# DeltaNet followed by soft MoE: products leave PSUM by ScalarE alone, masks are applied later in SBUF, both state copies run on ScalarE, and the routing exponentials are taken on transposed logits

## The chip, the cores and the metric

The kernel runs on one core of a Trainium2 chip. The metric is the device time of one execution in microseconds (us). Before the change three runs took 434.18, 437.84 and 441.81 us, so the median is 437.84.

## The reference

Two blocks stand one behind the other. The first is a DeltaNet recurrence over B = 4 batches, H = 8 heads, S = 768 steps and head size D = 48; for every batch and head it carries a 48x48 state:

```python
k_n = k / (norm(k, axis=-1) + 1e-6)
for t in range(S):
    y[t]  = q[t] @ state
    v_old = k_n[t] @ state
    state = state + beta[t] * outer(k_n[t], v[t] - v_old)
x = y as (B*S, H*D)                      # 3072 tokens x 384
```

The second is a soft mixture of experts on these 3072 tokens, with 8 experts of 4 slots each (32 slots) and a hidden size F = 1024:

```python
logits = x @ phi                                   # 3072 x 32
d = softmax over tokens of logits                  # per slot
slot_out = relu((d.T @ x)[expert e] @ w1[e]) @ w2[e]
c = softmax over slots of logits                   # per token
out = c @ slot_out                                 # 3072 x 384
```

## The kernel before

**Chunks and groups.** The recurrence is cut into 24 chunks of C = 32 steps. Within a chunk it is written as a small triangular system, so that only the state has to pass from chunk to chunk. Four chunks make a group (GC = 4, NG = 6 groups); the 128 partitions are 4 heads x 32 steps, and U = 8 pairs of a batch and a half of the heads lie side by side in the free dimension.

**What is done ahead of a chunk.** `prep(cc)` runs LEAD = 8 chunks ahead. It transposes K and Q on TensorE (L173) into PSUM, ScalarE copies them out (KQ, L176), and TensorE multiplies keys with keys and with queries (L188) into two PSUM banks. ScalarE takes the key-key half out (Lc, L194), and VectorE the query-key half, times the triangular mask `tri` (AT, L195). Once four chunks of a group are there, `invert(n)` solves their triangular systems together: VectorE transposes Lc into lb (L207), the norms follow (L221 to L229, with a square root on ScalarE), GpSimd scales lb (L230), and 31 elimination steps of two VectorE instructions each follow, a product pr (L240) and a subtraction from tt (L243). GpSimd scales tt (L247), and VectorE transposes it into TT (L253).

**A chunk itself.** TensorE multiplies the state with the keys (psR, L278), VectorE forms R = V - psR (L286), TensorE multiplies R with the inverse (psW, L297), ScalarE copies that to U (L300), TensorE adds to the state in PSUM (psS, L308), and the new state S is copied to SBUF in two halves: ScalarE takes the first (L320), VectorE the second (L318). The outputs (psY, L326) leave by ScalarE (Y, L329). GpSimd scales V two chunks ahead by the norms (L259).

**Routing.** After a group, `route` turns Y on TensorE (L350, copied by L351 to yT), forms logits (L359, copied to lT by L363), turns them to tokens (copied by VectorE to lg, L368), takes maxima and exponentials by slots and by tokens, and adds the weighted tokens to the running sum sacc (slots, L431 on TensorE and L439 on VectorE). One group's routing is spread over the four chunks of the next group.

**What sets the order.** Each engine executes its instructions in the order in which the program issues them, and between `tc.manual_schedule()` and its end that is the order of the code. A loop over x = -8 .. 23 issues, per chunk, `rest`, `scale_v`, `read`, then the pieces of `prep` and, between them, five places (PLACES = 5). Each place takes some elimination steps of the next group, as the table `share` gives them, and some steps of the routing:

```python
rest(); scale_v(x + 2); read()
x0(); place(0); solve(); x1(); place(1)
update(); outputs(); place(2); xp(); place(3); place(4)
```

**PSUM and queues.** Of the eight banks two belong to the tag pt (transposes, products, routing), one to psRW (psR and psW), one to psY and four to psS. K, Q and V are loaded over SyncE's queue, twelve chunks ahead for K and Q; Q of chunks 0 and 1 go over ScalarE's queue, beta and phi over GpSimd's.

**Behind the recurrence.** The expert weights w1 of experts 0 and 1 are loaded early. All others are issued by SyncE behind the recurrence (L152, L156), into buffers that use the recurrence's memory, so that each waits until that memory is free. First products (ph, L589) and second products (pso, L613) run over experts 0 to 3, then 4 to 7; then the output is formed and stored.

## Time and profile before

| what | value |
| --- | --- |
| median of 3 runs | 437.84 us (434.18 to 441.81) |
| the profiled execution's own time | 437.39 us |
| its span, first to last instruction | 435.7 us |
| mean granted TensorE clock | 0.855 |
| TensorE busy (matmuls / weight loads) | 299.1 / 227.6 us |
| VectorE busy | 248.9 us, 679 instructions |
| ScalarE busy | 129.1 us, 257 instructions |
| GpSimd busy | 63.5 us, 88 instructions |

The profile is that of one execution. A row of the groups view names the line of the code, the engine (PE is TensorE, PEld its weight loads, DVE VectorE, ACT ScalarE, POOL GpSimd, SP SyncE, SPq SyncE's queue of transfer issues), the operation, output and inputs with their shapes, the count, the busy time and the mean of one in ns, and the idle time ahead of them with what ended it. A waits row reads "who waited <- for whom: total us, times, longest". The span is 1.69 us shorter than the execution's own time.

### The profile page before, as it was taken

The numbers are of one execution on the slowest core, as the hardware profiler recorded it, in microseconds if no ns is written. First come the engines' busy times: TensorE is split into PE (matmuls) and PEld (weight loads), VectorE is DVE, ScalarE is ACT, GpSimd is POOL, SyncE is SP. The second block draws the span as 40 slices with busy tenths as digits, with TensorE's granted clock in tenths as the row PEclk, the third lists the DMA queues.
The fourth block names the chain that finished last, engine by engine and source line by source line (L and its number), as shares of the span: only waits on it lengthen the run. The fifth ranks groups of instructions, "written<-read, shape, count | busy, mean of one in ns | idle before, by whom it ended". The sixth has DMA issues, their size and how long they took to land. (4 is left out here: it accounts for less than half of the span.)

```text
span 435.7 us, 20600 instructions
## 1 busy us (share of the span) xinstructions
PE 299.1 (69%) x9387; PEld 227.6 (52%) x9387; DVE 248.9 (57%) x679; ACT 129.1 (30%) x257; POOL 63.5 (15%) x88
## 2 busy tenths in 40 slices
PE   3563547765686777857768767864777786887584
PEld 2452436654575656746656656654666664432142
DVE  4137978688868767586575875778752312111033
ACT  2242213233453224532154414323223221111022
POOL 8203034003300133000330013300130000000000
PEclk9999999799998697986699758867699697999695
DMA  6555955444432233223011100103100079879347
GB/s 109 98 90 88 320 83 86 76 83 81 71 54 37 43 58 59 42 43 53 4 21 24 21 10 16 22 3 105 46 5 5 3 245 428 346 294 426 148 152 283
DMA packets 84759, 45.53 MB, mean 105 GB/s; under 512 B 79392, under 2 KB 82624, under 8 KB 82624
## 3 DMA queue, kind: packets, MB, share of 16 engines
q1 hardware_dynamic: 81920, 43.67, 36.7%
q8 instruction: 74, 1.21, 1.1%
q10 hardware_dynamic: 2176, 0.39, 0.5%
q0 software_dynamic: 576, 0.15, 0.3%
q14 instruction: 13, 0.11, 0.1%
HBM read 39.47 MB, written 4.72 MB: 101 GB/s over the span
## 5 line engine op out<-in xcount | busy, mean ns | idle before, releaser
L240 DVE TENSOR_TENSOR pr<-tt,lb 128x31 f32<-128x31 f32 (+15 forms) x186 | 68.5, 368 | 9.5 <-POOL lb L230 4.7
L243 DVE TENSOR_TENSOR tt<-tt,pr 128x31 f32<-128x31 f32 (+15 forms) x186 | 68.2, 367 | 6.4
L173 PE MATMUL pt<-ident,K 128*128 128x128 f32 x96 | 34.3, 371 | 26.6 <-DVE AT L195 21.0
L176 ACT ACTIVATE KQ<-pt 128x512 f32<-128x512 f32 x48 | 28.5, 595 | 67.5 <-PE pt L173 67.5
L297 PE MATMUL psW<-R,TT 32*32 32x48 f32 x1536 | 25.8, 224 | 28.6 <-DVE R L286 28.0
L297 PEld LDWEIGHTS psW<-R,TT 32*32 32x32 f32 x1536 | 22.1, 122 | 34.4 <-DVE R L286 31.4
L318 DVE COPY S<-psS 48x768 f32<-48x768 f32 x23 | 22.1, 960 | 31.4 <-ACT S L320 31.4
L188 PE MATMUL pt<-KQ 48*32 48x64 f32 x1536 | 30.7, 263 | 11.9 <-issue 5.5
L173 PEld LDWEIGHTS pt<-ident,K 128*128 128x128 f32 x96 | 17.0, 178 | 32.7 <-DVE AT L195 23.3
L173 PE MATMUL pt<-ident,Q 128*128 128x128 f32 x96 | 32.2, 348 | 0.9 <-issue 0.9
L188 PEld LDWEIGHTS pt<-KQ 48*32 48x32 f32 x1536 | 21.9, 125 | 20.4 <-ACT KQ L176 8.7
L326 PE MATMUL psY<-U,AT 32*32 32x48 f32 x1536 | 26.4, 219 | 5.4 <-issue 5.3
L278 PE MATMUL psY<-S,KQ 128*32 128x96 f32 x768 | 28.8, 306 | 1.1 <-issue 1.1
L278 PE MATMUL psR<-S,KQ 128*32 128x96 f32 x768 | 29.4, 310 | 0.2
L431 PE MATMUL pt<-Y,dr 32*32 32x97 f32 x768 | 24.4, 278 | 6.7 <-issue 3.5
L247 POOL TENSOR_TENSOR tt<-tt,gm 128x1024 f32<-128x1024 f32 x6 | 11.5, 1912 | 103.0 <-DVE tt L243 89.9
L195 DVE TENSOR_TENSOR AT<-pt,tri 128x128 f32<-128x128 f32 x48 | 12.0, 289 | 25.0 <-ACT Lc L194 24.7
L326 PEld LDWEIGHTS psY<-U,AT 32*32 32x32 f32 x1536 | 21.8, 117 | 8.1 <-issue 6.4
L278 PEld LDWEIGHTS psY<-S,KQ 128*32 128x32 f32 x768 | 24.9, 144 | 1.5 <-issue 1.3
L278 PEld LDWEIGHTS psR<-S,KQ 128*32 128x32 f32 x768 | 23.1, 141 | 4.3 <-issue 2.6
L431 PEld LDWEIGHTS pt<-Y,dr 32*32 32x32 f32 x768 | 20.6, 123 | 9.1 <-issue 4.6
L194 ACT ACTIVATE Lc<-pt 128x128 f32<-128x128 f32 x48 | 14.6, 405 | 33.2 <-PE pt L188 33.2
(124 smaller groups left out, 440.4 us busy)
## 6 DMA issues: line engine op xcount, KB each, us to landing
w1t<-in_moe_w_dram SPq DMA_DIRECT2D x8, 1536.0 KB, 8.4
w2t<-in_moe_w_dram SPq DMA_DIRECT2D x8, 1536.0 KB, 14.1
K<-in_k_dram SPq DMA_DIRECT2D x96, 48.0 KB, 2.4
V<-in_v_dram SPq DMA_DIRECT2D x96, 48.0 KB, 2.3
out_dram<-ob SPq DMA_DIRECT2D x24, 192.0 KB, 2.3
Q<-in_q_dram SPq DMA_DIRECT2D x88, 48.0 KB, 2.7
Q<-in_q_dram ACTq DMA_DIRECT2D x8, 48.0 KB, 2.9
bb<-in_beta_dram POOLq DMA_DIRECT2D x16, 6.0 KB, 2.8
```

The costliest lines, as they stand in the source:

```text
L173: nc.tensor.transpose(tp[:, i, a, :], src[:, b * G:(b + 1) * G, :].rearrange("p g d -> p (g d)"), ident)
L176: nc.scalar.activation(KQ[cc][:, 2 * bh:2 * bh + 2], tp, ACT.Copy)
L188: nc.tensor.matmul(pg[g][rh, b], lhsT=KQ[cc][r, b, 0, rh], rhs=KQ[cc][r, b, :, rh], start=True, stop=True, skip_group_check=True)
L194: nc.scalar.activation(by[:, c, g], pg[g][:, :, 0, :], ACT.Copy)
L195: nc.vector.tensor_tensor(AT[cc][:, g], pg[g][:, :, 1, :], tri.unsqueeze(1).broadcast_to([P, B, C]), op=ALU.mult)
L240: nc.vector.tensor_tensor(prv, tt[:, j, 0:m].unsqueeze(1).broadcast_to([P, w, m]), lb[:, j, j + 1:C].unsqueeze(2).broadcast_to([P, w, m]), ...
L243: nc.vector.tensor_tensor(tt[:, j + 1:C, 0:m], tt[:, j + 1:C, 0:m], prv, op=ALU.subtract)
L278: nc.tensor.matmul(dst[hs[h], b].rearrange("p g d -> p (g d)"), lhsT=kq[:, b, a, hs[h]], rhs=old[:, h, b, :], start=(b == 0), stop=False, ...
L297: nc.tensor.matmul(pw[hs[h], u], lhsT=T[hs[h], u], rhs=st["R"][hs[h], u], start=(u == 0), stop=True, skip_group_check=True)
L318: nc.vector.tensor_copy(dst, src)
L326: nc.tensor.matmul(st["py"][hs[h], b, g], lhsT=at[hs[h], g, b], rhs=st["U"][hs[h], b * G + g], start=False, stop=True, skip_group_check=True)
L431: nc.tensor.matmul(pa[r], lhsT=st["dr"][r, c, b, :], rhs=Yn[r, c, b, 0:GD + 1], start=(b == 0), stop=(b == B - 1), skip_group_check=True)
```

## The change

- **Products and masks.** ScalarE copies both halves of the products together into a new tile GQ (128x256, two copies per chunk instead of two plus two). VectorE masks the query-key half later, in SBUF, with one instruction of 128x256 per chunk (`mask`, new L207), which is placed in the next chunk behind its first elimination steps.
- **State copies.** Both halves run on ScalarE (new L334).
- **Elimination.** The transpose to lb reads GQ with a stride and is issued at the end of the chunk before the group that it belongs to; the square root goes with it. GpSimd's scalings of lb and tt and the transpose to TT are each cut into two halves. `share` has four places per chunk, and the first chunk of a group takes 0.14 of the work (0.17 before), the next two 0.28 (0.31), the last 0.30 (0.23).
- **Routing.** Y is turned chunk by chunk (`turn`, four batches of one chunk, instead of one batch of four chunks), one chunk later. The maxima over tokens come from the transposed logits lT; the exponentials over tokens are taken on lT (dT) with the negative running maximum as bias, and those over slots straight from PSUM, with their sums by the same instruction (`accum_out`), four instructions of ScalarE. VectorE's copies and subtractions for them go. `slots` takes two chunks at a time.
- **Lead-in.** The eight steps x < 0 have a loop of their own. The order of the loads changes: Q1 moves from ScalarE's queue to SyncE's, K3 and Q3 from SyncE's to GpSimd's, and the masks are built ahead of beta and phi. A square root on a constant is put ahead of everything on ScalarE. Transposes in the lead-in use the banks psRW and psY.

```diff
+    one = cpool.tile([P, 1], F32, name="one")
+    nc.vector.memset(one, 1.0)
+    root = small.tile([P, 1], F32, name="root", tag="root", bufs=1)
+    nc.scalar.activation(root, one, ACT.Sqrt)
     load_k(0)
     load_q(0, nc.scalar)
-    load_k(1)
-    load_q(1, nc.scalar)
...
-    load_k(3)
-    load_q(3)
+    load_k(3, nc.gpsimd)
+    load_q(3, nc.gpsimd)
...
         def transposes(bh):
...
+            if cc < LEAD:
+                tag = ("psRW", "psY")[bh]
+                tp = ps.tile([P, 2, 2, P], F32, name="tp", tag=tag)
+            else:
+                tp = pt([P, 2, 2, P])
...
-            by = Lc[n].rearrange("p t (c b g) -> p c g b t", c=GC, b=B)
             for g in range(G):
-                nc.scalar.activation(by[:, c, g], pg[g][:, :, 0, :], ACT.Copy)
-                nc.vector.tensor_tensor(AT[cc][:, g], pg[g][:, :, 1, :],
-                                        tri.unsqueeze(1).broadcast_to([P, B, C]), op=ALU.mult)
+                nc.scalar.activation(GQ[n][:, c, :, g], pg[g], ACT.Copy)
+
+        def mask():
+            a = GQ[n][:, c, :, :, 1, :].rearrange("p b g t -> p (b g) t")
+            nc.vector.tensor_tensor(a, a, tri.unsqueeze(1).broadcast_to([P, U, C]), op=ALU.mult)
...
-            nc.vector.transpose(lb.rearrange("p t s -> p (t s)"),
-                                Lc.pop(n).rearrange("p t c -> p (t c)"))
+            nc.vector.transpose(
+                lb, GQ[n].rearrange("p c b g a t -> p a t (c b g)")[:, 0])
...
-            nc.gpsimd.tensor_tensor(st["lb"], st["lb"],
-                                    gm.unsqueeze(2).broadcast_to([P, C, C]), op=ALU.mult)
+            for r in (slice(0, C // 2), slice(C // 2, C)):
+                nc.gpsimd.tensor_tensor(
+                    st["lb"][:, r], st["lb"][:, r],
+                    gm[:, r].unsqueeze(2).broadcast_to([P, C // 2, C]), op=ALU.mult)
...
-                dst = new[r, :, :, g * D:(g + 1) * D]
-                src = psS[r, :, 0:B * D].rearrange("p h (b d) -> p h b d", d=D)
-                if g:
-                    nc.vector.tensor_copy(dst, src)
-                else:
-                    nc.scalar.activation(dst, src, ACT.Copy)
+                nc.scalar.activation(
+                    new[r, :, :, g * D:(g + 1) * D],
+                    psS[r, :, 0:B * D].rearrange("p h (b d) -> p h b d", d=D), ACT.Copy)
...
+        def over_slots():
...
+            nc.vector.tensor_reduce(mx, st["pq"], axis=AX.X, op=ALU.max, negate=True)
+            for b in range(B):
+                nc.scalar.activation(el[:, b], st["pq"][:, b], ACT.Exp, bias=mx[:, b:b + 1],
+                                     accum_out=sm[:, b:b + 1])
...
+        def spread_max():
...
+            dT = st["dT"] = wk.tile([P, P], F32, name="dT", tag="dT", bufs=1)
+            nc.scalar.activation(dT, st["lT"], ACT.Exp, bias=new)
...
-    PLACES = 5
+    PLACES = 4
-    share = [(0.0, 0.0, 0.05, 0.05, 0.07), (0.05, 0.06, 0.06, 0.06, 0.07),
-             (0.05, 0.06, 0.06, 0.06, 0.07), (0.08, 0.08, 0.07, 0.0, 0.0)]
+    share = [(0.0, 0.06, 0.06, 0.02), (0.10, 0.08, 0.08, 0.02),
+             (0.10, 0.08, 0.08, 0.02), (0.14, 0.10, 0.06, 0.0)]
...
         rest()
         scale_v(x + 2)
         read()
         x0()
+        if x > 0:
+            turn(i, Ys[m % 2], yT[m])
-        place(0)
+        drain(EL[c][0])
+        drain(masks)
         solve()
         x1()
+        routing[c][0][0]()
-        place(1)
+        drain(EL[c][1])
+        routing[c][0][1]()
         update()
         outputs()
-        place(2)
+        drain(EL[c][2])
         xp()
-        place(3)
-        place(4)
+        routing[c][1][0]()
+        drain(EL[c][3])
+        routing[c][1][1]()
+        masks = [mask]
+        if c == GC - 1 and n + 2 < NG:
+            spread, EL = plan(n + 2)
+            spread()
```

Three places show how the instructions move. The rows give the line, the operation, output and inputs and the shape; pr and tt are the elimination's two instructions.

**VectorE, second chunk of a group**, before: from R (in the first row) on through the state copy, the two masked products and the routing's copy lg.

```order
L286 TENSOR_TENSOR R<-V,psR 128x384
L240 TENSOR_TENSOR pr<-tt,lb 128x192
L243 TENSOR_TENSOR tt<-tt,pr 128x24x8
L240 TENSOR_TENSOR pr<-tt,lb 128x207
L243 TENSOR_TENSOR tt<-tt,pr 128x23x9
L240 TENSOR_TENSOR pr<-tt,lb 128x220
L243 TENSOR_TENSOR tt<-tt,pr 128x22x10
L318 COPY S_180<-psS 48x16x48
L240 TENSOR_TENSOR pr<-tt,lb 128x231
L243 TENSOR_TENSOR tt<-tt,pr 128x21x11
L195 TENSOR_TENSOR AT<-pt,tri 128x128 x2
```

Now, from R of the same chunk on (the mask L207, the routing's maximum over rows L409):

```order
L305 TENSOR_TENSOR R<-V,psR 128x384
L255 TENSOR_TENSOR pr<-tt,lb 128x175
L258 TENSOR_TENSOR tt<-tt,pr 128x25x7
L255 TENSOR_TENSOR pr<-tt,lb 128x192
L258 TENSOR_TENSOR tt<-tt,pr 128x24x8
L255 TENSOR_TENSOR pr<-tt,lb 128x207
L258 TENSOR_TENSOR tt<-tt,pr 128x23x9
L207 TENSOR_TENSOR GQ<-GQ,tri 128x8x32
L409 TENSOR_REDUCE mr<-pt 1x32
L255 TENSOR_TENSOR pr<-tt,lb 128x220
```

The state copy and the products out of PSUM are gone from VectorE's list; the mask, on SBUF alone, stands behind three elimination steps, ahead of a reduction that reads PSUM.

**ScalarE, the same chunk**, before (KQ and Lc of the chunk eight ahead, U, S and Y of this one, lT and yT of the routing):

```order
L176 ACTIVATE KQ<-pt 128x512
L300 ACTIVATE U<-psW 128x384
L176 ACTIVATE KQ<-pt 128x512
L351 ACTIVATE yT<-pt 96x4x4x32
L320 ACTIVATE S_180<-psS 48x16x48
L329 ACTIVATE Y_187<-psY 128x4x96
L363 ACTIVATE lT<-pt 128x128
L194 ACTIVATE Lc<-pt 128x4x32 x2
```

and now (el and sm are the exponentials over slots and their sums; ACT_TABLE_LOAD fetches another function's table):

```order
L186 ACTIVATE KQ<-pt 128x512
L361 ACTIVATE yT<-pt 96x16x32
L319 ACTIVATE U<-psW 128x384
L186 ACTIVATE KQ<-pt 128x512
L334 ACTIVATE S_184<-psS 48x16x48 x2
L345 ACTIVATE Y_192<-psY 128x4x96
L202 ACTIVATE GQ<-pt 128x4x64 x2
L393 ACT_TABLE_LOAD
L393 ACTIVATE el,sm<-pt,mx 128x32 x4
```

S has two copies in a row, GQ takes the place of Lc with twice the size, yT stands ahead of U, and four exponentials stand at the chunk's end.

**VectorE at a group's end**, before (sacc are the additions of the routing, TT the transposed inverse of the next group, R the first subtraction of that group, lb the transpose for the group after it):

```order
L240 TENSOR_TENSOR pr<-tt,lb 128x31
L243 TENSOR_TENSOR tt<-tt,pr 128x31
L439 TENSOR_TENSOR sacc<-sacc,pt 128x97
L195 TENSOR_TENSOR AT<-pt,tri 128x128 x2
L439 TENSOR_TENSOR sacc<-sacc,pt 128x97
L253 STREAM_TRANSPOSE TT<-tt 128x32x32
L439 TENSOR_TENSOR sacc<-sacc,pt 128x97
L286 TENSOR_TENSOR R<-V,psR 128x384
L207 STREAM_TRANSPOSE lb<-Lc 128x1024
L221 TENSOR_SCALAR ssq<-lb 128x32
```

and now:

```order
L255 TENSOR_TENSOR pr<-tt,lb 128x31
L258 TENSOR_TENSOR tt<-tt,pr 128x31
L272 STREAM_TRANSPOSE TT<-tt 128x16x32
L456 SCALAR_TENSOR_TENSOR sacc<-sacc,al,pt 128x97
L218 STREAM_TRANSPOSE lb<-GQ 128x1024
L229 TENSOR_SCALAR ssq<-lb 128x32
L305 TENSOR_TENSOR R<-V,psR 128x384
L236 RECIPROCAL rn<-nrm 128x32
```

Only half of TT stands behind the last elimination step (the first half is transposed a chunk earlier), and the transpose to lb with the squares ssq has moved from behind R to ahead of it.

More of the change, by code (lines that the diff above doesn't have):

```diff
@@ new lines, in shares, with over_rows @@
+        def shares():
+            sm = st["sm"]
+            nc.vector.tensor_scalar(sm, sm, 1e-9, None, op0=ALU.add)
+            nc.vector.reciprocal(sm, sm)
+            nc.gpsimd.tensor_tensor(Call[:, n], st["el"],
+                                    sm.unsqueeze(2).broadcast_to([P, B, NSL]), op=ALU.mult)
+        def over_rows():
+            pm = pt([1, B, NSL])
+            nc.tensor.transpose(pm.rearrange("p b s -> p (b s)"), st["m1"], ident)
+            mr = st["mr"] = small.tile([1, NSL], F32, name="mr", tag="mr")
+            nc.vector.tensor_reduce(mr, pm.rearrange("p b s -> p s b"), axis=AX.X, op=ALU.max)
@@ L388, in over_tokens @@
+        def spread_max():
+            pb = pt([P, 1])
+            for b in range(B):
+                nc.tensor.matmul(pb[C * b:C * b + C], lhsT=st["mr"], rhs=one[0:1],
+                                 start=True, stop=True, skip_group_check=True)
+            new, old = nrun[n % 2], nrun[1 - n % 2]
             if n == 0:
-                nc.vector.tensor_reduce(mrun, pm, axis=AX.X, op=ALU.max)
+                nc.vector.tensor_scalar(new, pb, -1.0, None, op0=ALU.mult)
             else:
-                m1 = small.tile([P, 1], F32, name="m1", tag="m1")
+                nc.vector.scalar_tensor_tensor(new, pb, -1.0, old, op0=ALU.mult, op1=ALU.min)
@@ L392, in over_tokens @@
                 al = st["al"] = small.tile([P, 1], F32, name="al", tag="al")
[L393 to L395 removed]
+                nc.vector.tensor_tensor(al, new, old, op=ALU.subtract)
                 nc.scalar.activation(al, al, ACT.Exp)
[L397 to L404 removed]
@@ L439, in slots @@
                 nc.vector.tensor_tensor(sacc, sacc, pa, op=ALU.add)
-        return ([lambda b=b: turn(b) for b in range(B)]
-                + [logits, by_tokens, maxima, over_tokens, shares, weights, repeat]
-                + [lambda c=c: slots(c) for c in range(GC)])
+        no = nothing
+        return [[(logits, no), (no, maxima)],
+                [(over_rows, no), (by_tokens, over_slots)],
+                [(no, no), (spread_max, shares)],
+                [(repeat, no), (lambda: slots((0, 1)), lambda: collect(True))],
+                [(no, no), (lambda: slots((2, 3)), lambda: collect(False))]]
+    nothing = lambda: None
     def drain(*lists):
```

268 lines of the change are left out of this document (142 added, 126 removed).

## The prediction

> **What bounds the kernel now.** I cut the span first into four stages, at VectorE's subtractions R (one per chunk of 32 steps), because every chunk of the recurrence passes through R. The rows of the windows view give, after start, end and length, the busy time and count on TensorE, its weight loads, VectorE, ScalarE and GpSimd, then the granted clock, the DMA share and GB/s.
>
> ```profile
> 0.00:64.50 64.50, 31.74 (x644) 24.48 (x644) 36.55 (x112) 17.56 (x36) 20.01 (x40) 1.00 0.64 132
> 64.50:322.30 257.80, 182.22 (x7116) 152.45 (x7116) 187.52 (x503) 87.63 (x170) 42.25 (x44) 0.82 0.24 45
> 322.30:348.80 26.50, 21.13 (x844) 17.80 (x848) 8.15 (x21) 9.30 (x18) 0.40 (x1) 0.84 0.01 4
> 348.80:435.70 86.90, 63.98 (x791) 32.88 (x783) 16.63 (x47) 14.61 (x33) 0.84 (x4) 0.85 0.74 291
> ```
>
> A, 64.5 us, is the lead-in up to the first R. B, 257.8 us, holds 20 chunks, during which the next group's elimination runs. C is three further intervals without elimination, D everything behind the last R. B decides. There VectorE is busy for 187.5 of 257.8 us and TensorE for 182.2, so neither is full, and the next question is what VectorE waits for. The waits view of stage B (total us, times, longest):
>
> ```profile
> DVE S L318 <- ACT S L320: 22.9, 19, 2.9
> DVE AT L195 <- ACT Lc L194: 12.4, 10, 2.4
> DVE R L286 <- PE psR L278: 9.8, 6, 2.2
> DVE TT L253 <- POOL tt L247: 4.0, 3, 1.7
> DVE sacc L439 <- PE pt L431: 3.6, 3, 1.4
> DVE rn L223 <- ACT nrm L222: 3.4, 5, 1.7
> DVE pr L240 <- POOL lb L230: 2.8, 4, 0.8
> PE psW L297 <- DVE R L286: 26.4, 10, 4.1
> ```
>
> VectorE's seven waits make 58.9 us; the remaining 11.4 us are the small gaps between its 503 instructions. It takes its list in order, so while it stands before the state copy S or the products AT, the elimination steps behind them stand too; so does the next R, for which TensorE in turn waits 26.4 us. That is my reading of B: VectorE's list, busy time plus waits, sets the pace. The chain that ended last reaches back only to 344.5 us and speaks for D alone.
>
> **B, part by part.** Durations come from the groups view (count | total us, mean ns | idle before):
>
> ```profile
> L318 DVE COPY S<-psS 48x768 f32<-48x768 f32 x23 | 22.1, 960 | 31.4 <-ACT S L320 31.4
> L320 ACT ACTIVATE S<-psS 48x768 f32<-48x768 f32 x23 | 18.5, 803 | 10.1 <-PE psS L308 9.7
> L195 DVE TENSOR_TENSOR AT<-pt,tri 128x128 f32<-128x128 f32 x48 | 12.0, 289 | 25.0 <-ACT Lc L194 24.7
> L240 DVE TENSOR_TENSOR pr<-tt,lb 128x256 f32<-128x256 f32 x6 | 2.5, 421 | 0.0
> L207 DVE STREAM_TRANSPOSE lb<-Lc 128x1024 f32<-128x1024 f32 x6 | 7.4, 1228 | 0.0
> L253 DVE STREAM_TRANSPOSE TT<-tt 128x1024 f32<-128x1024 f32 x6 | 11.8, 1961 | 4.0 <-POOL tt L247 4.0
> L439 DVE TENSOR_TENSOR sacc<-sacc,pt 128x97 f32<-128x97 f32 x18 | 4.5, 253 | 9.0 <-PE pt L431 8.7
> L397 DVE COPY mrun<-m 128x1 f32<-128x1 f32 x5 | 0.7, 147 | 0.1
> ```
>
> State copies: 20 x 0.960 = 19.2 us leave VectorE, and the wait of 22.9 us with them. On ScalarE both halves take 2 x 0.803 = 1.61 us, against 0.803 + 0.960 now, so the state is not later.
>
> Masks: 32 products of 0.289 us (9.2 us) go, with their wait of 12.4 us. In come 16 masks on 128x256 in SBUF, which no row shows; the elimination's 128x256 product at 0.421 is nearest, the two old products at 0.578 bound it above and one, 0.289, below. I take 0.421: 6.7 us, net -2.5 (-4.6 to 0). A mask is placed behind the next chunk's first elimination steps, when its copy is long done. ScalarE's copy doubles to 128x256, between its old 128x128 and a 128x512; it replaces two, so I add nothing.
>
> Routing: 17 groups of VectorE instructions, from L439 with the most time to L397 with the least, make 24.7 us for six groups, 4.1 each. Nine remain for each group; at a mean of 0.24 us, between 0.147 and 0.4, they make 2.2 (1.3 to 3.6). Four groups lie in B: -7.8 us (-11 to -2).
>
> The transpose to lb reads with a stride now. Contiguous it took 1.228, the transpose TT that writes with a stride 1.961; I take the slower: 4 x 1.96 - 5 x 1.23 = +1.7 us, since the one for group 1 moves into A (-1.2 to +4).
>
> Halves: GpSimd's scalings of lb and tt are cut in two so that VectorE starts after the first. Whether that gains is seen where GpSimd works beside VectorE:
>
> ```profile
> 224.37 1.62 POOL L259 TENSOR_TENSOR V<-V,nT 128x384 f32<-128x384 f32 x2
> 224.45 0.80 DVE L240 TENSOR_TENSOR pr<-tt,lb 128x31 f32<-128x31 f32 x1 [0.76 <-POOL lb L230]
> 60.19 0.19 DVE L240 TENSOR_TENSOR pr<-tt,lb 128x31 f32<-128x31 f32 x1
> ```
>
> The same product took 0.80 us beside GpSimd and 0.19 alone. A second half of about 1 us would hold VectorE up again; two such places in five groups cost 0 to 8 us, and I take 5. [...]
>
> Busy: 187.5 - 19.2 - 2.5 - 7.8 + 1.7 + 5 = 164.7 us. Gaps: about 440 instructions instead of 503, so 10. The waits for R, TT, sacc, rn and lb I keep: 23.6. That makes 198.3 us.
>
> What comes late next is R waiting for psR. How long a chunk takes without elimination is seen in C:
>
> ```profile
> 322.31 0.52 DVE L286 TENSOR_TENSOR R<-V,psR 128x384 f32<-128x384 f32 x1
> 328.37 0.56 DVE L286 TENSOR_TENSOR R<-V,psR 128x384 f32<-128x384 f32 x1 [1.27 <-PE psR L278]
> 337.83 0.56 DVE L286 TENSOR_TENSOR R<-V,psR 128x384 f32<-128x384 f32 x1
> 348.25 0.56 DVE L286 TENSOR_TENSOR R<-V,psR 128x384 f32<-128x384 f32 x1 [3.74 <-issue]
> ```
>
> So 6.1 to 10.4 us; I take 8. The list per chunk is 198.3 / 20 = 9.9 us on average and covers it, but the new shares put only 0.14 of the elimination into a group's first chunk, whose list comes to some 6.5 us: 1.5 us in five groups, 7.5 us. For the new reductions that wait for TensorE I add 2.2. **B: 208 us.** Its ends: 186, if halves cost nothing and half of the waits for TensorE go; 237, if the 35.3 us of S and AT come back before R and the halves cost 8.
>
> **A.** The queue rows carry this, with the first lb and the first elimination step:
>
> ```profile
> 0.81 7.57 SPq L80 DMA_DIRECT2D K<-in_k_dram  x12
> 8.42 1.93 SPq L80 DMA_DIRECT2D Q<-in_q_dram  x4
> 27.96 1.23 DVE L207 STREAM_TRANSPOSE lb<-Lc 128x1024 f32<-128x1024 f32 x1
> 35.28 0.80 DVE L240 TENSOR_TENSOR pr<-tt,lb 128x31 f32<-128x31 f32 x1 [1.91 <-POOL lb L230]
> ```
>
> SyncE issues twenty loads for chunks 0 to 2 instead of K0 to K3 and two Q; by these rows the last, Q2, is out at 0.81 + 7.57 + 2 x 1.93 = 12.2 us and lands, an estimate, near 15. K3 and Q3 go over GpSimd, ahead of beta, which is needed only for the norms. From 15 us I allow TensorE 10 for three chunks' transposes and products, now without the wait for the mask: lb at 25 instead of 28, and by the shorter norms (no table load, half a scaling) the first step at 30.3. From there it was 29.2 us to R; the transpose of group 1 (2.2) and the halves (1.6) come in, about 1 us of scaling goes: 32.2. **A: 62.5** (58 to 68; the upper end if GpSimd's eight issues delay what stands behind them).
>
> **C and D.** C loses turns and VectorE's copy: 24.5 (20.5 to 28.5). D is bound by weights:
>
> ```profile
> 355.14 2.13 SPq L156 DMA_DIRECT2D w2t<-in_moe_w_dram  x4
> 383.87 7.69 SPq L156 DMA_DIRECT2D w2t<-in_moe_w_dram  x4
> 391.18 17.68 DMA w2t<-in_moe_w_dram
> ```
>
> The last six loads wait for buffers that the first expert product frees, at 383, and land at 408.9, 25 us later; the loads before them are issued from 355.1, 7 us behind the last R. The routing chain after the recurrence has one turn instead of four and fewer VectorE steps, some 4 us less; but the earlier six loads need their 25 us too, from 7.5 us behind R, so the last lands no sooner than 57.5 behind it, against 60.6 now. **D: 83.8** (79 to 87).
>
> Sum: 62.5 + 208 + 24.5 + 83.8 = 378.8, and 1.7 us around the span, as now (437.39 - 435.70): **380 us**. The profiled 437.39 stands 0.45 below the median shown, 437.84, so nothing is corrected for.
>
> **Rivals.**
>
> TensorE at half clock remains the pace. For: it is busy as long as VectorE, and each long wait sends it to half clock:
>
> ```profile
> 275.37 0.88 PE L297 MATMUL psW<-R,TT 32*32 32x48 f32 x64
> 286.50 1.50 PE L297 MATMUL psW<-R,TT 32*32 32x48 f32 x64 [4.05 <-DVE R L286]
> ```
>
> The same 64 instructions took 1.50 after 4.05 us of idleness. Its work hardly shrinks: 182 us plus waits of 45 is B = 227, in all 400 us. Chance 0.18.
>
> TensorE stays at full clock. With 15 to 35 us fewer idle, chunks in the chain come nearer to 6.1 us, B falls to its lower end, 186, and the time to 358: 0.15. [...]
>
> The freed waits only change their name: R waits for psR as long as S and AT were waited for, and the masks, exponentials and ScalarE's longer queue take the rest. The work then brings nothing: 430 to 440 us, 0.04.
>
> Slower: ScalarE as the only exit from PSUM. Its exponentials stand ahead of the next chunk's KQ, yT and U, wait for a VectorE maximum, and hold the bank that TensorE's next turn needs, ahead of psW. Against: busy 87.6 + 20 x 0.803 + 3 = 107 us of 208. Slower by 2% needs 3.3 us more in each of 20 chunks; this place comes once in four. Then 447 and above, 0.03.
>
> **How the numbers follow.** The forecast case (362 to 398) has 0.60. The range 354 to 412 takes in most of the two cases beside it and leaves out some 0.17. About 2%, 9 us, is what a measurement here tells from no change: faster 0.93, same 0.04, slower 0.03.
>
> **What would show it.** VectorE's busy time over the whole span near 222 us instead of 248.9; no wait of VectorE for ScalarE's S; 20 chunks in about 208 us, a group's last the longest; granted clock above 0.82 there; first R near 62; last weights some 58 us after the last R. I am wrong if VectorE idles over 60 us in B (R before psR: chain or clock), if the mask or the strided transpose takes double, or if the first R comes after 68.

## The result and the profile after

The changed kernel takes 392.02 us (median of 4 runs, 390.32 to 394.22) against 437.45 us before. The ratio is 0.8987, with a 95% interval of 0.8909 to 0.9064. The profiled execution took 391.21 us, its span is 389.5. The ratios here and below are taken over the fast executions alone, so they differ a little from the quotient of the medians. The forecast was 380 us with a range of 354 to 412: right in direction, in size and in the range, but 12 us too low, and, as the experiments show, with the wrong pace-maker in the middle of the kernel. That the total came so near owes something to luck: the lead-in was forecast 4 us too long, the middle 10 and the tail 5 us too short.

The windows view of the kernel after, cut at the same places (first R, R of the 21st chunk, last R; columns as before: start and end, length, busy time and count of TensorE, its weight loads, VectorE, ScalarE, GpSimd, then granted clock, DMA share, GB/s):

```profile
0.00:58.45 58.45, 25.55 (x644) 19.54 (x644) 39.29 (x107) 16.24 (x37) 25.36 (x50) 0.76 0.75 141
58.45:276.58 218.13, 166.10 (x7090) 138.36 (x7091) 168.46 (x439) 110.61 (x222) 45.62 (x53) 0.90 0.30 54
276.58:300.56 23.98, 17.36 (x864) 14.43 (x866) 3.34 (x12) 11.51 (x26) 0.76 (x2) 0.98 0.02 5
300.56:389.50 88.94, 63.97 (x837) 34.20 (x828) 15.14 (x37) 14.99 (x39) 0.92 (x5) 0.85 0.71 284
```

| stage | before | forecast | after |
| --- | --- | --- | --- |
| A, to the first R | 64.5 | 62.5 | 58.45 |
| B, 20 chunks | 257.8 | 208 | 218.1 |
| C, three intervals | 26.5 | 24.5 | 24.0 |
| D, behind the last R | 86.9 | 83.8 | 88.9 |

The cut between C and D lies at the last R's end before (348.80) and at its start after; cut at its start (348.25), C and D before are 25.9 and 87.4. A ended 4 us earlier than forecast, B took 10 us more and D 5. What VectorE waited for in B, after (waits view; total us, times, longest):

```profile
DVE R L305 <- PE psR L297: 9.5, 6, 3.1
DVE TT L272 <- POOL tt L263: 5.8, 5, 1.2
DVE pr L255 <- POOL lb L244: 4.8, 5, 1.0
DVE sacc L456 <- PE pt L445: 3.8, 2, 2.1
DVE nrun L421 <- PE pt L415: 2.7, 2, 2.1
DVE sacc L459 <- PE pt L445: 2.6, 1, 2.6
DVE mr L409 <- PE pt L407: 2.3, 2, 1.6
DVE mx L391 <- PE pt L384: 2.2, 3, 1.2
DVE nrun L419 <- PE pt L415: 2.0, 1, 2.0
DVE R L305 <- DMA K<-in_k_dram: 1.9, 1, 1.9
```

The waits for S (22.9 us) and AT (12.4) are gone. With one more of 0.9 us these make 38.5; 168.5 busy and 38.5 waiting leave 11.1 us of small gaps, together 218.1. Of the 38.5 us, 26.0 are waits for TensorE (14.6 of 60.1 before). So the next view is what TensorE waits for in B, first of the kernel after:

```profile
PE psW L316 <- DVE R L305: 20.2, 5, 15.9
PE pt L198 <- issue: 16.8, 9, 2.5
PE psY L342 <- issue: 8.2, 7, 1.4
PE psR L297 <- issue: 3.5, 5, 1.1
PE psS L327 <- issue: 3.5, 5, 0.9
```

and the like rows of the kernel before:

```profile
PE pt L188 <- issue: 5.5, 5, 1.9
PE psY L326 <- issue: 4.7, 6, 1.3
PE pt L431 <- issue: 3.5, 3, 1.3
```

The longest wait of the first row, 15.9 us, ended just behind the first R and lies in the lead-in; what TensorE waits for R within B is some 4 us. "issue" is idle time for which the profile names no releaser. It made 18 us of TensorE's time in B before and makes 37 after (with the smaller rows). Where it falls is seen in stage C, where VectorE has nearly nothing to do: pieces of the chain that ended last, after (start, us, what):

```profile
281.20 1.62 issue
...
288.97 1.58 issue
...
293.83 0.60 issue
...
296.99 1.46 issue
```

Among the DMA queues the trace has two, q8 and q14, that it names as carrying instructions; their rows for stage C (packets, MB, share of 16 engines) are

```profile
q8 instruction: 7, 0.11, 1.7%
q14 instruction: 1, 0.01, 0.1%
```

Seven packets of q8 carry 0.11 MB, 16 KB each, while TensorE executes 864 matmuls and 866 weight loads: 247 recorded instructions to a packet. Over the whole span it is 74 packets to 18,846 recorded instructions of TensorE, 255 to a packet. The records of q8's single packets, set against the stops of TensorE and the count of its instructions between one unexplained stop and the next:

```
packet starts (us)     280.45          288.22          292.10          296.02
TensorE starts again   282.82          290.55          294.43          298.45
behind the packet        2.37            2.33            2.33            2.43
instructions since the last such stop
                          512             511             255             256
```

In C TensorE stops at every 256th or 512th instruction, to within one, and goes on 2.3 to 2.4 us behind a packet's start. In B of the changed kernel all 33 of its unexplained stops end 2.2 to 3.0 us behind a packet's start; of its 20 other waits there, one does. In B there are 55 packets, 3.3 to 5.3 us apart, median 3.8; before there were 56, 3.4 to 8.9 apart. That made theory F: TensorE's instruction supply, not VectorE's list (theory V), now sets the pace of B.

### The profile page after: what moved, and what is told of

Its sections match the earlier page's. It is cut to its first block, busy times and chain, and to the rows that moved or that the text cites. A ratio compares the mean times of both kernels' runs of the same rounds, so it can differ in the third digit from the quotient of the medians.

```text
span 389.5 us, 20669 instructions
## 1 busy us (share of the span) xinstructions
PE 273.0 (70%) x9423; PEld 206.5 (53%) x9423; DVE 226.2 (58%) x593; ACT 153.3 (39%) x322; POOL 72.7 (19%) x108
## 4 chain that ended last, share of the span: by engine, by line
PE 51%; issue 15%; DMA 13%; SPq 10%; DVE 5%; ACT 4%; POOL 1%; DVEq 0%; ACTq 0%; POOLq 0%
SPq L80 8%; PE pt L445 6%; PE psW L316 5%; PE psR L297 5%; PE psY L342 5%; DMA w2t<-in_moe_w_dram 5%; PE psS L327 5%; PE psY L297 4%; PE pt L183 4%; PE pt L198 4%; DMA Q<-in_q_dram 4%; PE pso L686 3%; DMA K<-in_k_dram 3%; PE pt L360 3%; PE ph L662 2%
## 5 line engine op out<-in xcount | busy, mean ns | idle before, releaser
L334 ACT ACTIVATE S<-psS 48x768 f32<-48x768 f32 x46 | 37.0, 805 | 16.8 <-PE psS L327 16.3
L263 POOL TENSOR_TENSOR tt<-tt,gm 128x512 f32<-128x512 f32 x12 | 13.6, 1133 | 143.7 <-DVE pr L255 79.5
L342 PE MATMUL psY<-U,GQ 32*32 32x48 f32 x1536 | 24.5, 206 | 14.7 <-issue 14.6
L316 PEld LDWEIGHTS psW<-R,TT 32*32 32x32 f32 x1536 | 19.2, 109 | 26.8 <-DVE R L305 22.4
L186 ACT ACTIVATE KQ<-pt 128x512 f32<-128x512 f32 x32 | 19.1, 596 | 35.0 <-PE pt L183 34.6
L198 PEld LDWEIGHTS pt<-KQ 48*32 48x32 f32 x1536 | 18.7, 111 | 22.4 <-issue 19.1
L445 PE MATMUL pt<-Y,dr 32*32 32x97 f32 x768 | 25.5, 292 | 6.2 <-issue 2.9
L342 PEld LDWEIGHTS psY<-U,GQ 32*32 32x32 f32 x1536 | 19.7, 107 | 17.6 <-issue 16.3
L445 PEld LDWEIGHTS pt<-Y,dr 32*32 32x32 f32 x768 | 22.2, 131 | 8.4 <-issue 4.0
L327 PE MATMUL psS<-U,K 32*48 32x48 f32 x1472 | 20.9, 218 | 6.6 <-issue 3.5
L327 PEld LDWEIGHTS psS<-U,K 32*48 32x48 f32 x1472 | 17.2, 120 | 12.3 <-issue 6.6
L202 ACT ACTIVATE GQ<-pt 128x256 f32<-128x256 f32 x48 | 15.8, 381 | 18.4 <-PE pt L198 18.3
L361 ACT ACTIVATE yT<-pt 96x512 f32<-96x512 f32 x24 | 14.1, 588 | 18.6 <-PE pt L360 18.6
L278 POOL TENSOR_TENSOR V<-V,nT 128x384 f32<-128x384 f32 x24 | 20.9, 881 | 0.9 <-DVE tt L258 0.7
```

The lines of the kernel that those rows point to most:

```text
L186: nc.scalar.activation(KQ[cc][:, 2 * bh:2 * bh + 2], tp, ACT.Copy)
L198: nc.tensor.matmul(pg[g][rh, b], lhsT=KQ[cc][r, b, 0, rh], rhs=KQ[cc][r, b, :, rh], start=True, stop=True, skip_group_check=True)
L278: nc.gpsimd.tensor_tensor(Vt[cc], Vt[cc], nT[n][:, c * U:(c + 1) * U].unsqueeze(2).broadcast_to([P, U, D]), op=ALU.mult)
L316: nc.tensor.matmul(pw[hs[h], u], lhsT=T[hs[h], u], rhs=st["R"][hs[h], u], start=(u == 0), stop=True, skip_group_check=True)
L327: nc.tensor.matmul(psS[DP * g:DP * g + D, h, b * D:(b + 1) * D], lhsT=K[hs[h], b * G + g, 0:D], rhs=st["U"][hs[h], b * G + g], start=(cc = ...
L334: nc.scalar.activation(new[r, :, :, g * D:(g + 1) * D], psS[r, :, 0:B * D].rearrange("p h (b d) -> p h b d", d=D), ACT.Copy)
```

## Experiments: what paces the kernel now

**Fewer TensorE instructions, output matmuls left out.**

```diff
         def outputs():
-            for b in range(B):
+            for b in range(0):
```

> The changed kernel without the 32 output matmuls of each chunk (psY, L342): the outputs Y then lack the part within the chunk. VectorE's and ScalarE's lists stay as they are. Theory V (VectorE's list paces stage B, as forecast): TensorE's work is beside it, B stays within 5 us of 218.1 and the time within 385 to 392. Theory F (TensorE's instruction supply paces B: in the changed kernel's trace 55 packets of 16 KB, 256 instructions each, reach it in B, 3.97 us apart on average, and it stands 37 us without a visible releaser): 128 of some 710 TensorE instructions per chunk go, 10 packets of 55, up to 40 us; VectorE's own list (168.5 busy, 11 of gaps, some 12 of waits for GpSimd) then holds B at about 192 to 200, so the time is 366 to 375. A theory of plain TensorE busy time gives 20 x 0.81 = 16 us less, 376.

362.44 us in one run, whose row for B is:

```profile
58.34:254.26 195.92, 147.88 (x5812) 123.18 (x5812) 167.70 (x439) 109.72 (x223) 45.65 (x53) 0.87 0.32 59
```

B fell to 195.9 with the same VectorE list (167.7 busy): 22 us less. V said at most 5 us, plain busy time 16, F a B of 192 to 200. TensorE's busy time fell by 18.2 us, so this run speaks against V but hardly tells F from plain busy time; the third edit does. The total lies 4 us below F's span, since C fell too, from 24.0 to 19.4 us.

**Less VectorE work, masks left out.**

```diff
         def mask():
-            a = GQ[n][:, c, :, :, 1, :].rearrange("p b g t -> p (b g) t")
-            nc.vector.tensor_tensor(a, a, tri.unsqueeze(1).broadcast_to([P, U, C]), op=ALU.mult)
+            return
```

> The changed kernel without its masks (L207): the products of queries with later keys stay in, so the outputs are those of an unmasked chunk. In stage B 17 instructions of 0.609 us go from VectorE's list, 10.4 us. Theory V: the time falls by 8 to 11 us, to 381 to 384. Theory F: VectorE is not what paces most chunks; 0 to 4 us, 388 to 392.

392.01 us, ratio 0.8918 (0.8869 to 0.8967): the same as the changed kernel. B is 217.3, and VectorE's wait for psR grew:

```profile
58.13:275.42 217.29, 166.00 (x7075) 137.95 (x7075) 163.76 (x422) 111.05 (x222) 44.90 (x53) 0.89 0.30 55
DVE R L304 <- PE psR L296: 11.2, 7, 4.8
```

VectorE's busy time in B fell by 4.7 us only, not by the 10.4 of the masks: other instructions now took longer (the product pr of 128x255 on average 0.754 us instead of 0.548). Of these 4.7 us B kept 0.8 as gain, and VectorE's waits grew from 38.5 to 41.7. Taking work from VectorE makes it wait longer, so V does not hold for most chunks.

**Fewer TensorE instructions, nothing left out.**

```diff
             for b in range(B):
-                for g in range(G):
-                    for h in range(4):
-                        nc.tensor.matmul(psS[DP * g:DP * g + D, h, b * D:(b + 1) * D],
-                                         lhsT=K[hs[h], b * G + g, 0:D],
-                                         rhs=st["U"][hs[h], b * G + g],
+                for h in range(4):
+                    bg = slice(b * G, (b + 1) * G)
+                    nc.tensor.matmul(psS[:, h, b * GD:(b + 1) * GD],
+                                     lhsT=K[hs[h], bg].rearrange("p g d -> p (g d)"),
+                                     rhs=st["U"][hs[h], bg].rearrange("p g d -> p (g d)"),
...
```

> The changed kernel with the state update in 16 matmuls of 32x128 by 32x96 per chunk instead of 32 of 32x48 by 32x48; the cross terms fall into PSUM columns that nobody reads, the result is the same. TensorE has 64 instructions fewer per chunk (9 per cent) for about the same array work; VectorE's and ScalarE's lists do not change. Theory F: 5 packets of 55 fewer in B, 3.97 us each, and 2 us in C: 370 to 378. Theory V: 388 to 392. If wide weights make the matmuls slower (in the rows of before 32 of 128x32 by 96 columns take 0.80 us, 64 of the small ones 0.83), the gain is smaller by up to 2 us per chunk, and the time could exceed 392.

373.99 us, ratio 0.8526 (0.8472 to 0.8580). B, and what TensorE stood for without a releaser in B (waits view), are

```profile
58.84:260.50 201.66, 165.32 (x6435) 137.35 (x6435) 168.67 (x440) 109.68 (x222) 45.63 (x53) 0.94 0.32 58
```

```profile
PE pt L198 <- issue: 5.4, 7, 1.1
PE psR L297 <- issue: 5.2, 6, 2.1
PE psW L316 <- issue: 2.9, 4, 1.1
```

TensorE was as busy as before this edit (165.3 against 166.1) and VectorE too (168.7 against 168.5), with 655 matmuls and as many weight loads fewer: 16 us less. The wide matmuls themselves cost more (0.293 us recorded for one, 28.6 in all, against 20.9 for the small ones), and ScalarE's state copies waited 21.0 us for the updates of all chunks instead of 16.3, so that step of the chain did not get shorter by it; it still paid. Nor is it the clock alone: the run without outputs had a lower one in B than the changed kernel, 0.87 against 0.90, and was 22 us faster there. What fell are the unexplained stops, from 37.0 to 19.1 us, and VectorE's waits, from 38.5 to 21.5. Of the theories here only the supply fits. Over the whole span q8 carried 68 packets instead of 74.

**The same edit in the kernel before.**

> The kernel before with the same merged state update. Its stage B was paced by VectorE's list, and TensorE stood 18 us there without a visible releaser, most of it beside VectorE's waits. Theory F says that the instruction supply became the pace only with the change: 430 to 438 here. If the supply had paced before as well, 5 packets of 56 at 4.6 us each would go: 415 to 420. Theory V: 434 to 438.

440.63 us against 439.75, ratio 1.0006 (0.9965 to 1.0048). That is 2.6 us above F's own span (430 to 438). In B of the profiled run TensorE's unexplained stops fell from 17.9 to 1.6 us, and B stayed, 258.5 against 257.8. There the supply was no limit: VectorE's waits left time for the packets, 56 in B before, 4.6 us apart on average, against 3.97 in the changed kernel. The change made the supply the bound, and these two runs, alike in the edit, show it.

## Experiments: where the gain came from

**State copies on ScalarE, alone, in the kernel before.**

```diff
-                if g:
-                    nc.vector.tensor_copy(dst, src)
-                else:
-                    nc.scalar.activation(dst, src, ACT.Copy)
+                nc.scalar.activation(dst, src, ACT.Copy)
```

> The kernel before with one part of the change alone: both state copies on ScalarE. In its stage B VectorE loses 19.2 us of copies and 22.9 us of waits. By the sum of the forecast (V alone) that would be up to 42 us, less what R and AT then wait longer: some 30, 405 to 412. By F the supply of 56 packets, which cannot come faster than the 3.97 us seen in the changed kernel, is a floor of 222 us for B: at most 36 us, so 402 at best, and VectorE still has masks from PSUM in its list, so 405 to 420. A rival: without the masks' change VectorE stands as long before AT, and the copy alone brings under 10 us, 428 to 438.

431.83 us, ratio 0.9858 (0.9806 to 0.9909). VectorE lost 22 us of work in B and the wait for S, but the wait for the products grew from 12.4 to 35.6 us:

```profile
DVE AT L195 <- ACT Lc L194: 35.6, 12, 5.7
```

That is the rival given in the expectation: the wait changed its name. F's floor of 222 us is an estimate from the mean distance of the packets in the changed kernel, 3.97 us; single ones came 3.3 us apart there, and no run shows that they cannot come faster.

**Masks in SBUF, alone, in the kernel before**, by the change's edits to products, mask and spread, with the mask behind the next chunk's first place:

```diff
             for g in range(G):
-                nc.scalar.activation(by[:, c, g], pg[g][:, :, 0, :], ACT.Copy)
-                nc.vector.tensor_tensor(AT[cc][:, g], pg[g][:, :, 1, :],
-                                        tri.unsqueeze(1).broadcast_to([P, B, C]), op=ALU.mult)
+                nc.scalar.activation(GQ[n][:, c, :, g], pg[g], ACT.Copy)
...
         place(0)
+        drain(masks)
+        masks = [mask]
         solve()
...
```

> The kernel before with another part alone: products leave PSUM by ScalarE into one tile, and the mask is applied a chunk later in SBUF (with the transpose to lb that reads with a stride). By the rows in B: 12.4 us of waits for Lc go, masks 32 x 0.289 become 20 x 0.609 (as measured in the changed kernel, plus 3), the transposes of lb cost 0.73 more each (plus 3): 5 to 8 us, 429 to 435. If the wait for S grows by what the wait for AT loses, nothing: 437 to 440.

429.34 us, ratio 0.9780 (0.9700 to 0.9861). A is 5 us shorter (59.3 instead of 64.5) and B 7, while D, cut at the last R's start, is 3 us longer. VectorE still waits for the state copy:

```profile
DVE S L318 <- ACT S L320: 18.5, 14, 2.6
```

**Both together in the kernel before.**

> The kernel before with both parts together, state copies on ScalarE and masks in SBUF; routing, shares, halves and lead-in as before. Each part alone brought 7 and 9 us, and each alone left the other's wait standing (the wait for Lc grew from 12.4 to 35.6 us when the state copy went). If the two waits stand in for each other, the two together bring much more than 16 us: B by the rows is 257.8 less 42.1 of state copies and their wait, less 12.4 of the wait for Lc, plus 6 of dearer masks and transposes, 209, held up by F to 222 and more; with A 59 and C 25 and D 88 the time is 394 to 404. If the parts simply add, 419 to 424, and the rest of the change (routing, shares, halves) made the other half of the gain.

413.32 us, ratio 0.9433 (0.9378 to 0.9488): 5.7% against 1.4 and 2.2 alone. The parts do more than add, but less than the sum of rows said (394 to 404). A is 59.8, D with 94.0 some 6.5 us longer than before, and B is 232.5; in it VectorE now waits for TensorE's routing steps as those stand in the old order:

```profile
DVE sacc L436 <- PE pt L428: 13.9, 8, 2.3
DVE lg L365 <- PE pt L364: 10.1, 4, 3.4
```

The two parts are thus worth some 24 us; the other 21 of the change come from the routing on transposed logits, the shares, the halves and the lead-in together, a difference that no run divides further except for the halves below.

**One part undone in the changed kernel**, the second half of the state copy back on VectorE:

```diff
-                nc.scalar.activation(
-                    new[r, :, :, g * D:(g + 1) * D],
-                    psS[r, :, 0:B * D].rearrange("p h (b d) -> p h b d", d=D), ACT.Copy)
+                dst = new[r, :, :, g * D:(g + 1) * D]
+                src = psS[r, :, 0:B * D].rearrange("p h (b d) -> p h b d", d=D)
+                if g:
+                    nc.vector.tensor_copy(dst, src)
+                else:
+                    nc.scalar.activation(dst, src, ACT.Copy)
```

> The changed kernel with the second half of the state copy back on VectorE. If VectorE had no slack in it, its list gains 20 x 0.96 and up to 23 us of waiting for ScalarE's half: 392 plus 19 to 42, so 411 to 434. By F the list has some slack (leaving the mask's 10.4 us out changed nothing), and the first 10 us are free: 400 to 425.

399.64 us, ratio 0.9125 (0.9051 to 0.9199), B 226.2. That is below the span without slack (411 to 434) and just below F's (400 to 425). VectorE is 20 us busier in B and B 8 us longer, so some 12 of the 20 us found slack in VectorE's list, and the list stands close behind the supply. The wait for ScalarE's half that was so long before is 1.4 us here: in the changed order VectorE has more elimination steps ahead of the copy (in this trace five per chunk on average between R and the copy, in that of before 2.75).

```profile
DVE S L337 <- ACT S L339: 1.4, 2, 0.7
```

The mask back to PSUM on VectorE:

```diff
-                nc.scalar.activation(GQ[n][:, c, :, g], pg[g], ACT.Copy)
+                nc.scalar.activation(GQ[n][:, c, :, g, 0], pg[g][:, :, 0, :], ACT.Copy)
+                nc.vector.tensor_tensor(GQ[n][:, c, :, g, 1], pg[g][:, :, 1, :],
+                                        tri.unsqueeze(1).broadcast_to([P, B, C]), op=ALU.mult)
...
```

> The changed kernel with the mask taken by VectorE straight from PSUM, as before, and the key half alone by ScalarE. VectorE's list changes by 32 x 0.289 less 17 x 0.609, minus 1 us, and gains waits for TensorE and ScalarE, 12 us in the kernel before. By V: 392 plus 8 to 12, 400 to 404. By F the supply paces most chunks, and VectorE's slack takes the wait up: 390 to 398.

401.21 us, ratio 0.9144 (0.9081 to 0.9208). The wait is back with 17.1 us, and B is 223.6, 5.5 us longer; another 2 us are lost in A, 1.3 in C and 1.5 in D. The time lies in V's span (400 to 404) and above F's (390 to 398). In B, where both theories speak, the loss is 5.5 us, less than V's 8 to 12 and within F's 6 at most: the slack took up a part of the wait, not all of it. This run does not decide between them.

```profile
DVE GQ L203 <- ACT GQ L202: 17.1, 13, 3.2
```

The halves undone (one scaling of lb, one of tt, one transpose TT):

```diff
-            for r in (slice(0, C // 2), slice(C // 2, C)):
-                nc.gpsimd.tensor_tensor(
-                    st["lb"][:, r], st["lb"][:, r],
-                    gm[:, r].unsqueeze(2).broadcast_to([P, C // 2, C]), op=ALU.mult)
+            nc.gpsimd.tensor_tensor(st["lb"], st["lb"],
+                                    gm.unsqueeze(2).broadcast_to([P, C, C]), op=ALU.mult)
...
```

> The changed kernel without the halves: one scaling of lb and of tt on GpSimd, one transpose TT, at the group's end. The forecast priced the halves at 5 us of VectorE blocked by GpSimd in B and nothing gained. If that holds and VectorE's time counted, 386 to 392. [...]

396.94 us, ratio 0.9078 (0.9017 to 0.9139), above the expectation's 386 to 392; by time alone that is not clear of the changed kernel. B is 223.5 in the profile, and the waits that the halves had shortened are back, TT 5.8 to 10.4 and lb 4.8 to 9.1:

```profile
DVE TT L269 <- POOL tt L261: 10.4, 5, 2.1
DVE pr L253 <- POOL lb L243: 9.1, 5, 1.9
```

So by the profiles the halves save some 5 us; the forecast had counted them as 5 us lost.

## Experiments: the tail

Weight issues on SyncE's queue in the kernel after, and two pieces of its chain:

```profile
301.19 0.35 SPq L157 DMA_DIRECT2D w1t<-in_moe_w_dram  x1
314.48 1.92 SPq L161 DMA_DIRECT2D w2t<-in_moe_w_dram  x4
316.45 20.48 SPq L157 DMA_DIRECT2D w1t<-in_moe_w_dram  x4
336.98 7.63 SPq L161 DMA_DIRECT2D w2t<-in_moe_w_dram  x4
```

```profile
305.45 3.35 issue
...
344.22 18.52 DMA w2t<-in_moe_w_dram
```

Behind one load at 301.19, six loads (four of w2, two of w1) are issued from 314.48 on, 13.9 us behind the last R (300.56); before it was 6.9. SyncE's queue waits there 12.9 us for TensorE's L445: slots, the last routing step of group 4, reads that group's outputs until 314. The last six loads follow from 336.12 on (within the third row), when the first expert product has ended. TensorE also stands 3.35 us at 305.45, 511 instructions behind its last such stop, while a weight load is under way. The first edit moves the last group's routing up by one chunk:

```diff
-        routing[c][0][0]()
+        last = n == NG - 1
+        early = c + 1 if last and c >= 2 else c
+        routing[early][0][0]()
...
-    late = routing[-1]
-    late[1][0]()
-    late[1][1]()
```

> The changed kernel with the last routing steps of group 4 (slots and before it repeat, over shares and maxima) issued one chunk earlier in the last group, so that nothing of group 4 stands behind the last R. Six weight loads wait for the memory that these steps read: they were issued 13.9 us behind the last R instead of 6.9 before the change. If that is what made D longer than forecast, the loads go out 6 to 7 us earlier and TensorE's tail loses two slots (4 us): D 84 to 86 instead of 88.9, C 1 to 3 us longer, 386 to 390 in all. If D is bound by the second six loads alone, which wait for the first expert product, only the two slots count: 388 to 391. If neither, 392.

Its last slots still stand behind the last R, since they run at the last chunk's end. 395.36 us, ratio 0.9059 (0.8981 to 0.9136), above all three spans of the expectation. The six loads go out from 9.8 us behind R, but D is 88.4, and C 28.3. Four us earlier brought half a us in D and lost 4 in C: the last six loads wait for the first expert product, and the first of them goes out 35.3 us behind R here, 35.6 in the changed kernel.

**All of it moved, with the merged update.** All routing of group 4 ahead of the last R; w2 of experts 4 and 5 ahead of w1 of 6 and 7 in SyncE's order; `repeat` in wide matmuls, for which dT holds four copies:

```diff
...
-                for h in range(4):
-                    nc.tensor.matmul(pd[C * h:C * h + C, c].rearrange("p b s -> p (b s)"),
-                                     lhsT=st["dT"][:, C * c:C * c + C], rhs=ident,
+                nc.tensor.matmul(pd[:, c].rearrange("p b s -> p (b s)"),
+                                 lhsT=st["dT"][:, c].rearrange("p h t -> p (h t)"), rhs=ident,
...
-    for e in range(E):
-        if e >= NW1:
+    for first_w1, w1s, w2s in ((0, (2, 3), (0, 1, 2, 3)), (1, (4, 5), (4, 5)), (2, (6, 7), (6, 7))):
+        for e in w1s:
             load_w1(e, wp2, 4)
-        if e % 4 == 3:
-            for i in range(e - 3, e + 1):
-                load_w2(i, wp2, 6)
+        for e in w2s:
+            load_w2(e, wp2, 6)
```

> The changed kernel with the merged state update of the earlier run (374.0), with repeat in 4 wide matmuls instead of 16 (48 TensorE instructions fewer per group and one wider exponential on ScalarE), with all routing of group 4 issued ahead of the last R, and with w2 of experts 4 and 5 loaded ahead of w1 of experts 6 and 7. The result is the same. By F the 48 instructions are a fifth of a packet per group, at most 1 us each: B 198 to 202. If D is bound by the stream of weights, which ran at 420 to 430 GB/s from 14 us behind the last R until its end: twelve loads of 1.57 MB take 44 us, and with the start at about 2 to 5 us behind R the last lands near 52 behind it instead of 62.2: D 79 to 82, C 3 to 4 us longer by the two slots, 364 to 369 in all. If the first expert product (36 us behind R) gates the last loads whatever was issued before them, D stays at 86 to 89 and the time at 372 to 377. A rival against it: weights that run from the last R on delay TensorE's instruction packets (a hole of 3.35 us there in the changed kernel) in every step of the last routing: 2 us at each of 3 packets, D 86.

365.65 us, ratio 0.8352 (0.8292 to 0.8413), the fastest of the kernels that leave nothing out. Its last stage and its weight issues:

```profile
282.69:359.90 77.21, 57.35 (x649) 28.77 (x637) 14.55 (x35) 14.69 (x38) 0.83 (x4) 0.88 0.80 327
```

```profile
283.32 0.35 SPq L157 DMA_DIRECT2D w1t<-in_moe_w_dram  x1
283.76 4.21 SPq L161 DMA_DIRECT2D w2t<-in_moe_w_dram  x4
```

Weights stream from 0.6 us behind the last R, and D is 77.2 instead of 88.9, below the 79 to 82 expected. Behind the load at 283.32 seven more of thirteen are out 7.1 us behind R, and the last weights land 52.6 us behind it instead of 62.2. How much of this is the order of the loads and how much the routing moved ahead, no run divides. B is 200.05 there, 1.6 us under the run with the merged update alone.

## Why the prediction was right or wrong, point by point

- **State copies and masks.** That the waits for S and AT go was right. That both must go together the forecast left unsaid: alone they brought 1.4 and 2.2%, because VectorE then waits for the other. The rival "the waits only change their name" was given 0.04 for the whole change; for one part alone it is what happens.
- **Price of the mask.** 0.421 us was taken from the elimination's product. Alone it takes 0.42, beside GpSimd 1.27 (timeline of the kernel after):

```profile
69.99 0.42 DVE L207 TENSOR_TENSOR GQ<-GQ,tri 128x256 f32<-128x256 f32 x1
79.78 1.22 POOL L263 TENSOR_TENSOR tt<-tt,gm 128x512 f32<-128x512 f32 x1 [14.51 <-DMA K<-in_k_dram]
80.01 1.27 DVE L207 TENSOR_TENSOR GQ<-GQ,tri 128x256 f32<-128x256 f32 x1
```

  The mean became 0.609, 10.4 us in B instead of 6.7. In this pair the mask began 0.23 us behind the start of GpSimd's scaling of tt and ended 0.28 us behind its end. Why it took longer there, the runs do not show.
- **Other VectorE terms.** The strided transpose to lb took 1.954 against 1.96 taken; routing 7.7 us against 8.8; the elimination rose from 114.4 to 118.8 us, 4.4 against 5 taken for GpSimd's halves. VectorE's busy time in B came to 168.5 against 164.7.
- **The halves.** The sign was wrong. What VectorE loses beside GpSimd was priced at 5 us, an estimate from one pair of rows (a product of 128x31 took 0.80 us beside GpSimd and 0.19 alone), and no run shows that term by itself: VectorE is busy for 161.2 us in B without the halves and for 168.5 with them, 7.2 more. The shorter waits at a group's end were not priced; the run without halves shows these to be worth more: its waits for GpSimd in B are 19.6 us against 10.6.
- **What paces B.** This step failed. The forecast let VectorE's list cover the chain in all chunks but a group's first, and added 2.2 us for the new reductions. Its sum fell short by 3.8 us of busy time, 1 of gaps and 5 of waits (38.5 against 33.3 allowed). That the waits came so near was luck, since they stand in other places: the reductions waited 9.2 us for TensorE, R 9.5 (of 17 allowed). With 9% fewer TensorE instructions R's wait is

```profile
DVE R L305 <- PE psR L297: 2.9, 4, 1.2
```

  though neither engine is less busy. The rival "TensorE stays at full clock", 358, had the clock about right (granted 0.90 in B, 0.94 with the merged update) and missed the supply. The half-clock rival, 400, came closer in number than the forecast and was wrong in mechanism: the granted clock in B rose from 0.82 to 0.90. For its premise, half clock at each long wait, the trace of before has six waits for R in B of 2.55 to 4.05 us, at each of which a stretch with a granted clock of 0.50 began between 1.0 us ahead of the wait's end and 1.1 us behind it; at three of 1.4 to 2.2 us none began (the clock's records start at 70.45 us). Of the signs named, no wait for ScalarE's S came true, and VectorE's 49.6 us of idleness in B stayed under the 60 that would have meant the forecast was wrong: that sign did not see the supply. The "issue" rows were in the waits view of before, 18 us, and were not asked about.
- **A.** The first lb stood at 21.5 instead of 25 and the first elimination step at 27.2 instead of 30.3. The last load that the forecast counted, Q2, landed at 14.5, as estimated; lb followed 7 us behind it instead of 10. The run with the masks alone, with the loads in the old order, reaches A = 59.3: most of the gain came with the masks, and all else, with ScalarE's table load of 1.28 us at 2.77 instead of 29.66 (ahead of the first square root in both), is about 1 us.
- **C** came as forecast. **D** did not; two terms failed. "From 7.5 us behind R" was 13.9, because the forecast took the order of before for what frees the memory, although slots of group 4 had moved behind the last chunk. And the routing chain, counted 4 us shorter, was not: the first expert product began 27.6 us behind R against 26.8 before, with TensorE's stop of 3.35 us on the way, so the last weights landed 62.2 us behind R against 60.6. The run with the loads 4 us earlier, D 88.4, shows that the first term alone was not the bound.

## What to carry to other kernels

When an engine's waits are removed, ask of the engine that delivers to it not only how long it is busy but how many instructions it executes: here TensorE executes some 710 small instructions per chunk, its packets of 256 never came closer than 3.3 us in B, and merging matmuls gained 18 us though they took longer. An "issue" row in the waits can be a bound in waiting, although its 18 us before the change cost nothing: count the instructions between two such stops. Waits that stand in for each other must be removed together, and a part that brings 2% alone can be worth more beside another.

## What the hardware showed that was not expected

In the trace of the changed kernel q8 carried 74 packets of 16 KB to 18,846 recorded instructions of TensorE, 255 to a packet, and in C TensorE stopped 255, 256, 511 and 512 instructions behind the stop before; that is read here as packets of 256 of its instructions. In the 218 us of B the packets were never closer than 3.3 us, and after its unexplained stops TensorE resumed 2.2 to 3.0 us behind a packet's start, in C 2.3 to 2.4. While a weight load was under way one such stop lasted 3.35 us; its packet started 6.8 us behind the one before it, and TensorE went on 2.5 us behind that start. That the load delayed the packet is not shown. A matmul of 32x128 by 96 columns was recorded with 0.293 us against 0.218 for one of 32x48 by 48, and does the work of two. Why the packets keep that distance, the runs do not show.
